# A decode block on one core: w_out's last rows cut into other lanes, x loaded row by row

## The chip, the core and the metric

The kernel runs on one core of a Trainium2 chip. The metric is the device time in microseconds. Before the change its median over three runs is 662.07 us (661.95 to 662.16).

## The reference

A decode step for four sequences (B = 4, one new token each, D = 640). The normalised x feeds two branches whose results are added to x: attention over a cache of 4,096 positions with 32 heads of 128, and a gated MLP with F = 1728, Fh = 864.

```python
def _A_ref(x, k_cache, v_cache, wq, wo):          # caches: (4, 32, 4096, 128) bf16
    q = (x @ wq).reshape(B, 1, 32, 128).transpose(0, 2, 1, 3)
    scores = jnp.einsum('bhqd,bhkd->bhqk', q, k) * Dh ** (-0.5)
    p = _softmax(scores, axis=-1)
    o = jnp.einsum('bhqk,bhkd->bhqd', p, v)
    return o.transpose(0, 2, 1, 3).reshape(B, 1, 4096) @ wo

def _B_ref(x, w_in, w_sp, b_sp, w_out):
    z = _gelu(jnp.einsum('bsd,df->bsf', x, w_in))
    z1, z2 = z[..., :Fh], _layernorm(z[..., Fh:], axis=-1)
    g = jnp.einsum('ts,bsf->btf', w_sp, z2) + b_sp[None, :, None]
    return jnp.einsum('bsf,fd->bsd', z1 * g, w_out)   # w_out: (864, 640)

xn = _layernorm(x, axis=-1)
return x + _A_ref(xn, k_cache, v_cache, wq, wo) + _B_ref(xn, w_in, w_sp, b_sp, w_out)
```

The two caches are 134 MB each; together with the weights 282 MB have to come in from HBM.

## The kernel before

**Units.** Attention is cut into NU = 16 units: a group of 8 heads of one sequence, 8 x 4096 rows of 128 as 128 partitions x 256 rows. A unit's k is 8.4 MB and its v as much. A unit's k is worked on in NK = 4 quarters of 64 rows per partition. The ring (`k_ring`) has 7 such places, `v_all` holds one unit's v.

**Steps.** For each quarter n: `product(n)` (L537) multiplies k by q on VectorE, `fold_half(n)` (L543) adds the halves, `sums(n)` (L555) lets TensorE add up the rest through the identity, `row_sums` (L569) finishes a score row. At the first quarter of the next unit come `head_max` (L578 to L588), `exps` (L596, ScalarE) and `by_head` (L607). `weighted` (L631) multiplies v by the probabilities. After every fourth unit `group_turn` and `group_proj` (L672 to L699) multiply by w_o into `out_ps`, where x and the MLP's result are summed as well.

**Loads.** All of them but x, w_sp and b_sp go out on SyncE's DMA queue, in the order of the list `loads` (L195). `pump()` issues the next one as soon as its places in ring or `v_all` are free by the program's order; the semaphores then hold it on the chip until the last reader is done. The list starts: wq (L118), k of unit 0 in quarters 0 and 1 (L164), `load_w` (w_in, L127, and w_out's parts with t = 1, L124), k of unit 0 in quarters 2 and 3, `load_w_few` (w_out's part with t > 1), k of unit 1. From there v and k alternate. Every DMA of the program, SyncE's and ScalarE's alike, takes one of eight semaphores in turn, so a DMA also waits until the one eight places earlier has landed.

**w_out.** `W_OUT` (L62) cuts its 864 rows into parts (partitions, rows per partition, transfers): 128 partitions of five rows (800 KB, in `v_all`), 128 of one row (160 KB) and 12 partitions, here called lanes, of eight rows (10,240 bytes each). The lanes go in four transfers of three lanes: `w[l:n:t]` with t = 4. `w_rows` lists the 14 row sets (NFC) with their first row, partitions and step.

**x.** One transfer of four rows on ScalarE's queue (L101), w_sp and b_sp after the first q (L735, L736).

**MLP.** `gmlp()` is a generator whose steps are called in the first two quarters: the products with w_in (L404), a copy of PSUM for each run of parts with the same number of partitions (`by_lanes`, L414), GELU, layer norm and gate (L418 to L500), and the products with w_out (L503), which read all parts. V of unit 0 (L175) is loaded into `v_all` after them.

**The end.** The last unit's v comes in two halves, the second cut into 32, 16, 8, 8 rows (`V_CUTS`), then w_o of the last group in six pieces (L228, L231); the last products (L809, L699), a copy on ScalarE (L823) and two transfers out (L824, L825) follow.

Of the kernel before, what the change touches and what calls it, by code (L numbers as in the profile page):

```python
# [10 lines left out]
BF16 = mybir.dt.bfloat16  # L11
# [6 lines left out]
def kernel(  # L18
# [14 lines left out]
    nc = tc.nc  # L33
    P = nc.NUM_PARTITIONS
    Bsz, Sq, D = A_x.shape
    _, H, S, Dh = A_k_cache.shape
    HD = A_wq.shape[1]
    F = B_w_in.shape[1]
    Fh = F // 2
# [19 lines left out]
    RW = 8  # L59
    QW = HC * Dh  # L60
    RING = 2 * NK - 1
    W_OUT = ((P, 5, 1), (P, 1, 1), (12, 8, 4))  # L62
    assert sum(n * r for n, r, _ in W_OUT) == Fh
    NFC = sum(r for _, r, _ in W_OUT)

    def up(n):
        return -(-n // 256) * 256

    PW = sum(up(r * D) for _, r, _ in W_OUT[1:])
    NOH = D // 2  # L70
    CB = 4
    NG = NR // CB
# [8 lines left out]
    const = ctx.enter_context(tc.tile_pool(name="const", bufs=1))  # L81
# [16 lines left out]

    ring = places.tile([P, RING, QW], BF16, name="k_ring")
    x_bf = ring[0:Bsz, 1, 0:D]  # L100
    nc.scalar.dma_start(out=x_bf, in_=A_x.flatten_outer_dims())  # L101
    v_all = places.tile([P, NK * QW], BF16, name="v_all")

    wq_sb = v_all[:, 0 : DC * HD].rearrange("p (c n) -> p c n", c=DC)
# [2 lines left out]

    at_v = up(DC * (HD + F))
    w_parts, f0, at_p = [], 0, 0
    for n, r, t in W_OUT:  # L110
        if f0 == 0:
            room = v_all[0:n, at_v : at_v + r * D]
        else:
            room = p_buf[0:n, at_p : at_p + r * D]
            at_p += up(r * D)
        w_parts.append((room.rearrange("p (k n) -> p k n", k=r), f0, n, r, t))
        f0 += n * r
    nc.sync.dma_start(out=wq_sb, in_=A_wq.rearrange("(p c) n -> p c n", c=DC))  # L118

    def load_part(part):  # L120
        w, f0, n, r, t = part
        rows = B_w_out[f0 : f0 + n * r].rearrange("(p k) n -> p k n", k=r)
        for l in range(t):
            nc.sync.dma_start(out=w[l:n:t], in_=rows[l:n:t])  # L124

    def load_w():
        nc.sync.dma_start(out=w_in_sb, in_=B_w_in.rearrange("(p c) n -> p c n", c=DC))  # L127
        for part in w_parts:
            if part[4] == 1:
                load_part(part)  # L130

    def load_w_few():
        for part in w_parts:
            if part[4] > 1:
                load_part(part)

    w_rows = [
        (w[:, i], f0 + i, n, r) for w, f0, n, r, _ in w_parts for i in range(r)
    ]

    def run_of(cache, u):
# [101 lines left out]
    for e in range(PAR):  # L243
        nc.gpsimd.tensor_copy(
            out=of_row[:, e, :, :, e, :],
            in_=ident[:].rearrange("p (k q) -> p q k", q=QD)[:, 0:Bsz, :, None].to_broadcast(
                [P, Bsz, NQ, LN]
            ),
# [15 lines left out]
    for i in range(NSTAT):  # L264
# [5 lines left out]
        out=rstd[:], in_=mv[:, 1:2], func=ACT.Sqrt, bias=eps_tile[:Bsz], scale=1.0  # L270
# [4 lines left out]
        out=xn_bf,  # L275
# [4 lines left out]
        op1=ALU.mult,  # L280
    )

    wsp_bf = const.tile([1, 1], BF16)
    bsp_bf = const.tile([1, 1], BF16)

    xn_v = xn_bf.rearrange("b (p c) -> b c p", c=DC)
    xnT_ps = ps_m.tile([P, DC, Bsz], BF16, tag="m")
    for c in range(DC):
        nc.tensor.transpose(
            out=xnT_ps[:, c, :], in_=xn_v[:, c, :], identity=ident[:Bsz, :Bsz]  # L290
# [8 lines left out]
    for e in range(PAR):  # L299
        q_ps = ps_pv.tile([P, HG, Dh], FP32, tag="pv", name="q_ps")  # L300
        for c in range(DC):
            for k in range(NQ):
                nc.tensor.matmul(  # L303
                    out=q_ps[k * QD : (k + 1) * QD],
# [5 lines left out]
        rows = const.tile([P, HG, Dh], BF16, name=f"q_rows{e}")  # L310
        nc.vector.tensor_scalar(  # L311
            out=rows[:], in0=q_ps[:], scalar1=scale_qk, scalar2=None, op0=ALU.mult
# [7 lines left out]
        out=hot[:].rearrange("p c h -> p (c h)"),  # L320
        in_=ident[:].rearrange("p (g m) -> p m g", m=QD),
# [6 lines left out]
        out=pick[:, :, Bsz - 1 :].rearrange("p c (k q) -> p c k q", q=QD)[  # L328
            :, :, :, 0 : PAR * Bsz : Bsz
        ],  # L330
        in_=hot[:].rearrange("p c (k e) -> p c k e", e=PAR),
# [4 lines left out]
        out=of_set[:],  # L336
        in_=hot[:].rearrange("p c h -> p (c h)")[:, 0 : PAR * Bsz].rearrange(
            "p (e b) -> p e b", b=Bsz
        ),
# [5 lines left out]
    with nc.allow_low_precision("0 and 1"):  # L345
        nc.vector.tensor_reduce(
            out=own[:],
            in_=ident[:].rearrange("p (h l) -> p h l", h=HT),
# [5 lines left out]
        out=par[:], in_=own[:].rearrange("p (k e) -> p e k", e=PAR), axis=AX.X, op=ALU.add  # L354
# [3 lines left out]
        out=far[:],  # L358
# [13 lines left out]
    for half in range(2):  # L372
        nc.tensor.matmul(
            out=out_ps[OG * half : OG * half + OG, :],
# [7 lines left out]
    for name in ("zz", "gw", "gt"):  # L382
        gm[name] = work.tile([P, 2, NFC, Bsz], FP32, name=name)
    gm["gz"] = work.tile([P, 3, NFC, Bsz], FP32, name="gz")
    nc.gpsimd.memset(gm["zz"][:], 0.0)
    gm["st"] = work.tile([1, 5 * Bsz], FP32, name="st")
    gm["ac"] = work.tile([1, 2 * Bsz], FP32, name="ac")
    gm["yT"] = work.tile([P, NFC, Bsz], BF16, name="yT")

    by_lanes = []  # L390
    for n, r, _ in W_OUT:
        if by_lanes and by_lanes[-1][0] == n:
            by_lanes[-1] = (n, by_lanes[-1][1] + r)
        else:
            by_lanes.append((n, r))

    def gmlp():
        zz, gw, gt, gz = (gm[n] for n in ("zz", "gw", "gt", "gz"))
        zT = ps_pv.tile([P, 2, NFC, Bsz], FP32, tag="pv", name="zT")
        for t in range(2):  # L400
# [331 lines left out]
    E = mybir.EngineType  # L732
    with tc.manual_schedule(engines={E.PE, E.DVE, E.Activation, E.SP}):
        stage_q(0)
        nc.scalar.dma_start(out=wsp_bf[:], in_=B_w_sp[0:1, 0:1])  # L735
        nc.scalar.dma_start(out=bsp_bf[:], in_=B_b_sp[0:1].rearrange("(a b) -> a b", a=1))  # L736
        waiting = None
        mlp = gmlp()
        for n in range(NK * NU):
            u, i = divmod(n, NK)  # L740
            product(n)
            if n and n % 2 == 0:
                row_sums(n - 1)
            if i == 0 and u:
                head_max(u - 1)
                if waiting in taken:
                    picked(waiting)
            fold_half(n)
            if n == 1:
                next(mlp)  # L750
                next(mlp)
            if i == 0 and u:
                exps(u - 1)
                if waiting in pvs:
                    take(waiting)
                by_head(u - 1)
            sums(n)
            if i == 0 and u + 1 < NU:
                stage_q(u + 1)
            if i == 0 and waiting is not None:  # L760
                if waiting in taken:
                    picked(waiting)
                if waiting % Bsz == Bsz - 1:
                    group_turn(waiting // Bsz)
                    group_proj(waiting // Bsz)
                waiting = None
            if n == 0:
                next(mlp)
            if n == 1:
                next(mlp)  # L770
                next(mlp)
                next(mlp)
                busy.remove(V)
            if n in turns:
                w = waiting = turns[n]
                if w % Bsz == Bsz - 1:
                    group_den(w // Bsz)
                if w == NU - 3:
                    weighted(w, v_runs[:, 0:NC], more=True)
                    weighted(w, v_runs[:, NC:NR], NG // 2)  # L780
                else:
                    weighted(w, v_runs)
                if i < NK - 1:
                    take(w)
                busy.remove(V)
            pump()
        weighted(NU - 2, v_runs)
        row_sums(NK * NU - 1)
        head_max(NU - 1)
        exps(NU - 1)  # L790
        take(NU - 2)
        by_head(NU - 1)
        den = ps_m.tile([P, NQ, PAR, Bsz], FP32, tag="m", name="den_all")
        nc.tensor.matmul(
            out=den[:],
            lhsT=ones_sq[:],
            rhs=acc[(HG - 1) % NACC][:, :, 0 : PAR * Bsz],
            start=True,
            stop=True,
        )  # L800
        rden = small.tile([P, NQ, PAR, Bsz], FP32, name="rden_all")
        nc.vector.reciprocal(out=rden[:], in_=den[:])
        picked(NU - 2)
        u, b = NU - 1, Bsz - 1
        weighted(u, v_ends[0])
        take(u)
        pick_last(u, more=True)
        for c in range(NC):
            nc.tensor.matmul(  # L809
                out=o_last[0][:, :, :, b],  # L810
                lhsT=v_ends[1][:, c, :],
                rhs=p_m[:, u % 2, NG // 2 + c // CB, c % CB, :].rearrange("p (k e) -> p k e", e=PAR),
                start=False,
                stop=(c == NC - 1),
            )
        o_n = small.tile([P, NQ, PAR, Bsz], BF16, name="o_n_last")
        nc.vector.tensor_tensor(out=o_n[:], in0=o_last[0][:], in1=rden[:], op=ALU.mult)  # L817
        gr[HG - 1] = [o_n[:, h // PAR, h % PAR, :] for h in range(HT)]
        group_proj(HG - 1)

        res = v_all[:, 0:NOH]
        out_v = out.flatten_outer_dims()
        nc.scalar.copy(out=res[0 : OG + Bsz], in_=out_ps[0 : OG + Bsz])  # L823
        nc.scalar.dma_start(out=out_v[:, 0:NOH], in_=res[0:Bsz])  # L824
        nc.sync.dma_start(out=out_v[:, NOH:D], in_=res[OG : OG + Bsz])  # L825
# [30 lines left out]
```

## Time and profile before

| what | us |
|---|---|
| median of three runs | 662.07 |
| the profiled execution's own time | 662.09 |
| its span, from first to last instruction | 660.2 |
| VectorE busy | 522.6 |
| TensorE busy (granted clock 0.692 over the span) | 317.0 |
| SyncE's queue, share of the 16 DMA engines | 99.1% |
| VectorE waiting for k before `product` | 87.9, in 13 waits, the longest 7.6 |
| issue of a whole unit's k to its landing, median | 27.2 |
| the same for v | 32.6 |

"Busy" is the time in which an engine worked on an instruction; issues of DMAs and semaphore work are not in it. The page also slices the span into 40 parts; the DMA's row, in tenths, is 9 in each but the last:

```profile
DMA  9999999999999999999999999999999999999997
GB/s 369 433 461 434 417 441 434 433 437 438 421 445 426 437 430 441 437 422 433 434 441 441 418 437 441 430 441 421 434 441 437 426 421 445 422 427 436 449 409 284
```

### The profile page before, as it was taken

What the parts mean: (1) busy time and instruction counts of PE and PEld (TensorE: products, weight loads), DVE (VectorE), ACT (ScalarE), POOL (GpSimd) and SP (SyncE); (2) the same over time, 40 slices, a digit from 0 to 9 for tenths busy, and PEclk for the clock granted to TensorE, in tenths of its full rate; (3) what the DMA queues carried; (4) which work ended last, traced back from release to release, by engine and by line L of the source; (5) the groups of instructions that cost most, each with busy time, mean ns of one, the idle gap of its engine ahead of it and who ended that gap; (6) DMA issues with size and microseconds to landing.
All of it is one profiled execution on the core that took longest, in us unless ns stands there. A gap on an engine that the chain in (4) does not pass through costs nothing.

```text
span 660.2 us, 4777 instructions
## 1 busy us (share of the span) xinstructions
PE 317.0 (48%) x2083; PEld 136.3 (21%) x2083; DVE 522.6 (79%) x276; ACT 29.9 (5%) x73; POOL 10.1 (2%) x20
## 2 busy tenths in 40 slices
PE   0574372526427363452636336263452534737367
PEld 0231121212213121120212112121120211212124
DVE  1767978959597795969959598695969969999950
ACT  0020000000000000000000000000000000000000
POOL 2300000000000000000000000000000000000000
PEclk9757676766767676585767768676685867676785
DMA  9999999999999999999999999999999999999997
GB/s 369 433 461 434 417 441 434 433 437 438 421 445 426 437 430 441 437 422 433 434 441 441 418 437 441 430 441 421 434 441 437 426 421 445 422 427 436 449 409 284
DMA packets 8232, 282.55 MB, mean 428 GB/s; under 512 B 892, under 2 KB 2184, under 8 KB 2568
## 3 DMA queue, kind: packets, MB, share of 16 engines
q1 hardware_dynamic: 8192, 282.25, 99.1%
q8 instruction: 16, 0.26, 0.1%
q10 hardware_dynamic: 20, 0.01, 0.0%
q14 instruction: 4, 0.03, 0.0%
HBM read 282.24 MB, written 0.01 MB: 428 GB/s over the span
## 4 chain that ended last, share of the span: by engine, by line
DMA 62%; DVE 28%; PE 8%; issue 1%; ACT 0%; DVEq 0%
DMA k_ring<-in_A_k_cache_dram 53%; DVE k_ring L537 14%; DVE k_ring L543 7%; PE s_ps L555 6%; DMA v_all<-in_A_v_cache_dram 4%; DMA k_ring<-in_A_wo_dram 3%; DVE s_sb L569 3%; DMA v_all<-in_A_wq_dram 2%; DVE p_m L607 1%; DVE m L578 1%; PE q_ps L303 1%; PE pv L631 1%; PE out_ps L699 1%; DVE p_m L678 1%; DVE mf L580 1%
## 5 line engine op out<-in xcount | busy, mean ns | idle before, releaser
L537 DVE TENSOR_TENSOR k_ring<-k_ring,qbc 128x8192 bf16<-128x8192 bf16 x64 | 282.9, 4420 | 88.5 <-DMA k_ring<-in_A_k_cache_dram 87.9
L555 PE MATMUL s_ps<-k_ring,ident 128*128 128x512 bf16 x512 | 202.2, 566 | 313.8 <-DVE k_ring L543 313.7
L555 PEld LDWEIGHTS <-ident 128*128 128x128 bf16 x512 | 64.0, 130 | 430.0 <-issue 245.4
L543 DVE TENSOR_TENSOR k_ring<-k_ring 128x4096 bf16<-128x4096 bf16 x64 | 145.9, 2280 | 1.1
L631 PE MATMUL pv<-v_all,p_m 128*32 128x512 bf16 x960 | 62.5, 419 | 0.0
L569 DVE TENSOR_REDUCE s_sb<-s_ps 128x128 f32<-128x1024 f32 x32 | 39.0, 1218 | 3.7 <-PE s_ps L555 3.7
L607 DVE TENSOR_TENSOR p_m<-p_c,own 128x2048 bf16<-128x2048 bf16 x16 | 36.6, 2285 | 0.7 <-ACT p_c L596 0.7
L631 PEld LDWEIGHTS <-p_m 128*32 128x32 bf16 x992 | 26.6, 106 | 42.5 <-issue 23.3
L596 ACT ACTIVATE p_c<-s_sb,nm 128x256 bf16<-128x256 f32 x16 | 8.1, 508 | 342.9 <-DVE nm L588 342.9
L662 PEld LDWEIGHTS o_ps<-o_rows,pick 128*128 128x128 f32 x96 | 20.4, 294 | 4.3 <-issue 3.3
L662 PE MATMUL o_ps<-o_rows,pick 128*128 128x128 f32 x96 | 19.1, 367 | 0.0
L643 ACT COPY o_rows<-pv 128x512 f32<-128x512 f32 x16 | 9.4, 586 | 165.7 <-PE pv L631 165.7
L311 DVE TENSOR_SCALAR q_rows<-q_ps 128x512 bf16<-128x512 f32 x2 | 1.4, 692 | 12.8 <-PE q_ps L303 12.8
L817 DVE TENSOR_TENSOR o_n_last<-o_last,rden_all 128x32 bf16<-128x32 f32 x1 | 0.2, 192 | 12.2 <-PE o_last L809 12.2
L303 PE MATMUL q_ps<-v_all,xnT 128*32 128x512 bf16 x40 | 4.5, 630 | 9.3 <-DMA v_all<-in_A_wq_dram 9.3
L527 ACT CAST qbc<-qbc_ps 128x128 bf16<-128x128 f32 x16 | 4.3, 266 | 97.6 <-PE qbc_ps L519 97.6
L578 DVE TENSOR_REDUCE m<-s_sb 128x1 f32<-128x256 f32 x16 | 6.7, 420 | 0.5
L519 PE MATMUL qbc_ps<-q_rows,of_row 128*128 128x128 bf16 x32 | 6.0, 276 | 0.6 <-DVE q_rows L311 0.6
L519 PEld LDWEIGHTS <-of_row 128*128 128x128 bf16 x32 | 4.1, 132 | 8.1 <-issue 7.4
L716 PE MATMUL o_last<-hot,o_rows 128*128 128x8 f32 x32 | 4.9, 279 | 0.7 <-ACT o_rows L643 0.7
L716 PEld LDWEIGHTS o_last<-hot,o_rows 128*128 128x128 f32 x32 | 4.8, 226 | 1.8 <-ACT o_rows L643 1.6
L699 PE MATMUL out_ps<-k_ring,p_m 128*4 128x320 bf16 x48 | 4.0, 309 | 2.1 <-DVE p_m L691 2.1
(87 smaller groups left out, 81.4 us busy)
## 6 DMA issues: line engine op xcount, KB each, us to landing
k_ring<-in_A_k_cache_dram SPq DMA_DIRECT2D x5, 4096.0 KB, 27.2
v_all<-in_A_v_cache_dram SPq DMA_DIRECT2D x2, 4096.0 KB, 28.2
v_all<-in_A_wq_dram SPq DMA_DIRECT2D x1, 5120.0 KB, 15.4
k_ring<-in_A_k_cache_dram SPq DMA_DIRECT2D x2, 2048.0 KB
k_ring<-in_A_v_cache_dram SPq DMA_DIRECT2D x1, 4096.0 KB
k_ring<-in_A_wo_dram SPq DMA_DIRECT2D x3, 1280.0 KB, 20.6
v_all<-in_B_w_in_dram SPq DMA_DIRECT2D x1, 2160.0 KB
k_ring<-in_A_v_cache_dram SPq DMA_DIRECT2D x1, 2048.0 KB
```

The lines of the kernel that those rows point to most:

```text
L303: nc.tensor.matmul(out=q_ps[k * QD : (k + 1) * QD], lhsT=xnT[:, c, :], rhs=wq_v[:, c, k, e], start=(c == 0), stop=(c == DC - 1),)
L519: nc.tensor.matmul(out=qb_ps[:], lhsT=of_row[:, e, b].rearrange("p k f l -> p (k f l)"), rhs=q_rows[e][:, hg, :], start=(e == 0), stop=(e ...
L537: nc.vector.tensor_tensor(out=t, in0=t, in1=qbcs[u][:, None, :].to_broadcast([P, HC, Dh]), op=ALU.mult)
L543: nc.vector.tensor_tensor(out=t[:, :, 0:HD2], in0=t[:, :, 0:HD2], in1=t[:, :, HD2:Dh], op=ALU.add)
L555: nc.tensor.matmul(out=s, lhsT=ident[:], rhs=t[:, :, g * RW : (g + 1) * RW], start=(g == 0), stop=(g == m - 1),)
L569: nc.vector.tensor_reduce(out=scores[u][:].rearrange("p (r c) -> p r c", r=NK)[:, lo : hi + 1 : hi - lo], in_=sums_ps.pop(n // 2)[:], axis ...
L578: nc.vector.tensor_reduce(out=m1[:], in_=scores[u][:], axis=AX.X, op=ALU.max)
L607: nc.vector.tensor_tensor(out=p_m[:, u % 2], in0=p_c.pop(u)[:].rearrange("p (g c) -> p g c", c=CB)[:, :, :, None].to_broadcast([P, NG, CB, HT]
L631: nc.tensor.matmul(out=pvs[u][cg * QD : (cg + 1) * QD, :], lhsT=p_m[:, u % 2, g0 + n].rearrange("p c h -> p (c h)"), rhs=v_at[:, n * CB : ...
L662: nc.tensor.matmul(out=gr[hg][:], lhsT=pick[:, c, Bsz - 1 - b : P + Bsz - 1 - b], rhs=o[:, c, :], start=(b == 0 and c == 0), stop=(b == Bs ...
L699: nc.tensor.matmul(out=out_sum(half), lhsT=o, rhs=wo_sb[:, n, half * NOH : (half + 1) * NOH], start=False, stop=(hg == HG - 1 and n == HT ...
L716: nc.tensor.matmul(out=o_last[0][:, :, :, u % Bsz], lhsT=o[:, c, :], rhs=hot[:, c, :].rearrange("p (k e) -> p k e", e=PAR), start=(c == 0) ...
```

## The change

`W_OUT` gets three other parts: 128 partitions of five rows as before, 24 partitions of one row, and 25 lanes of eight rows. A part now lists its transfers as (when, first lane, number of lanes, step): "wide" ones go out with `load_w`, "few" ones with `load_w_few`, and lane 22 goes in two halves of four rows, one with each. So 128 rows in one transfer and 96 rows in four become 24 rows in three transfers (12, 8 and 4 lanes) and 200 rows in eight: with `load_w` one of five lanes and half a lane, with `load_w_few` two of five, three of three and the other half lane. NFC stays 14. The flag `near` is true in every part, so each partition's rows stay neighbours in HBM.

x is loaded in four transfers of one row. The loads of w_sp and b_sp move from after the first q to right behind x on ScalarE's queue. `by_lanes` now has three runs of parts, so the copy at L414 is made three times. The steps of the MLP stand as they were, and so does everything behind it.

On SyncE's queue six transfers come in, four ahead of k's quarters 2 and 3 and two ahead of unit 1's k. With three more on ScalarE's, the turn of the eight semaphores moves, so the early loads wait for others than before: k's quarter 1 for x's first row, w_in for wq, the first half lane for k's quarter 0, k's quarters 2 and 3 for quarter 1, the six small transfers after it for w_in, w_out's five rows, and the 12-, 8-, 4- and 5-lane transfers, k of unit 1 for the first half lane.

```diff
-    W_OUT = ((P, 5, 1), (P, 1, 1), (12, 8, 4))
-    assert sum(n * r for n, r, _ in W_OUT) == Fh
-    NFC = sum(r for _, r, _ in W_OUT)
+    W_OUT = (
+        (P, 5, True, (("wide", 0, 128, 1),)),
+        (24, 1, True, (("wide", 0, 12, 1), ("wide", 12, 8, 1), ("wide", 20, 4, 1))),
+        (25, 8, True, (("wide", 1, 5, 4), ("few", 2, 5, 4), ("few", 7, 5, 4), ("few", 0, 3, 4), ("few", 3, 3, 9), ("few", 16, 3, 4), ("half", 22, 1, 1))),
+    )
+    assert sum(n * r for n, r, _, _ in W_OUT) == Fh
+    NFC = sum(r for _, r, _, _ in W_OUT)
...
-    nc.scalar.dma_start(out=x_bf, in_=A_x.flatten_outer_dims())
+    x_rows = A_x.flatten_outer_dims()
+    for b0, b1 in ((0, 1), (1, 2), (2, 3), (3, 4)):
+        nc.scalar.dma_start(out=x_bf[b0:b1], in_=x_rows[b0:b1])
+    wsp_bf = const.tile([1, 1], BF16)
+    bsp_bf = const.tile([1, 1], BF16)
+    nc.scalar.dma_start(out=wsp_bf[:], in_=B_w_sp[0:1, 0:1])
+    nc.scalar.dma_start(out=bsp_bf[:], in_=B_b_sp[0:1].rearrange("(a b) -> a b", a=1))
...
-    def load_part(part):
-        w, f0, n, r, t = part
-        rows = B_w_out[f0 : f0 + n * r].rearrange("(p k) n -> p k n", k=r)
-        for l in range(t):
-            nc.sync.dma_start(out=w[l:n:t], in_=rows[l:n:t])
+    def load_part(part, on):
+        w, f0, n, r, near, cuts = part
+        rows = B_w_out[f0 : f0 + n * r].rearrange(
+            "(p k) n -> p k n" if near else "(k p) n -> p k n", k=r
+        )
+        for kind, l, m, step in cuts:
+            if kind == on:
+                end = l + (m - 1) * step + 1
+                nc.sync.dma_start(out=w[l:end:step], in_=rows[l:end:step])
+            if kind == "half":
+                part_r = slice(0, r // 2) if on == "wide" else slice(r // 2, r)
+                nc.sync.dma_start(out=w[l : l + m, part_r], in_=rows[l : l + m, part_r])
 
     def load_w():
         nc.sync.dma_start(out=w_in_sb, in_=B_w_in.rearrange("(p c) n -> p c n", c=DC))
         for part in w_parts:
-            if part[4] == 1:
-                load_part(part)
+            load_part(part, "wide")
 
     def load_w_few():
         for part in w_parts:
-            if part[4] > 1:
-                load_part(part)
+            load_part(part, "few")
...
     w_rows = [
-        (w[:, i], f0 + i, n, r) for w, f0, n, r, _ in w_parts for i in range(r)
+        (w[:, i], f0 + i * (1 if near else n), n, r if near else 1)
+        for w, f0, n, r, near, _ in w_parts
+        for i in range(r)
     ]
...
         stage_q(0)
-        nc.scalar.dma_start(out=wsp_bf[:], in_=B_w_sp[0:1, 0:1])
-        nc.scalar.dma_start(out=bsp_bf[:], in_=B_b_sp[0:1].rearrange("(a b) -> a b", a=1))
```

More of the change, by code (lines that the diff above doesn't have):

```diff
@@ L61 @@
     RING = 2 * NK - 1
-    W_OUT = ((P, 5, 1), (P, 1, 1), (12, 8, 4))
-    assert sum(n * r for n, r, _ in W_OUT) == Fh
-    NFC = sum(r for _, r, _ in W_OUT)
+    W_OUT = (
[5 more added lines that the diff above has]
+    NFC = sum(r for _, r, _, _ in W_OUT)
     def up(n):
         return -(-n // 256) * 256
-    PW = sum(up(r * D) for _, r, _ in W_OUT[1:])
+    PW = sum(up(r * D) for _, r, _, _ in W_OUT[1:])
     NOH = D // 2
@@ L109 @@
     w_parts, f0, at_p = [], 0, 0
-    for n, r, t in W_OUT:
+    for n, r, near, cuts in W_OUT:
         if f0 == 0:
@@ L115 @@
             at_p += up(r * D)
-        w_parts.append((room.rearrange("p (k n) -> p k n", k=r), f0, n, r, t))
+        w_parts.append((room.rearrange("p (k n) -> p k n", k=r), f0, n, r, near, cuts))
         f0 += n * r
     nc.sync.dma_start(out=wq_sb, in_=A_wq.rearrange("(p c) n -> p c n", c=DC))
-    def load_part(part):
-        w, f0, n, r, t = part
-        rows = B_w_out[f0 : f0 + n * r].rearrange("(p k) n -> p k n", k=r)
-        for l in range(t):
-            nc.sync.dma_start(out=w[l:n:t], in_=rows[l:n:t])
+    def load_part(part, on):
[10 more added lines that the diff above has]
+                nc.sync.dma_start(out=w[l : l + m, part_r], in_=rows[l : l + m, part_r])
     def load_w():
@@ L281 @@
     )
-    wsp_bf = const.tile([1, 1], BF16)
-    bsp_bf = const.tile([1, 1], BF16)
     xn_v = xn_bf.rearrange("b (p c) -> b c p", c=DC)
@@ L390 @@
     by_lanes = []
-    for n, r, _ in W_OUT:
+    for n, r, _, _ in W_OUT:
         if by_lanes and by_lanes[-1][0] == n:
```

## The prediction

> **What bounds the kernel now.** I read the page's totals, then the chain that ended last, then SyncE's issues, then stretches of the span.
>
> ```profile
> span 660.2 us, 4777 instructions
> PE 317.0 (48%) x2083; PEld 136.3 (21%) x2083; DVE 522.6 (79%) x276; ACT 29.9 (5%) x73; POOL 10.1 (2%) x20
> DMA packets 8232, 282.55 MB, mean 428 GB/s; under 512 B 892, under 2 KB 2184, under 8 KB 2568
> q1 hardware_dynamic: 8192, 282.25, 99.1%
> q8 instruction: 16, 0.26, 0.1%
> ```
>
> VectorE is busy for 79%, but the one queue that SyncE feeds keeps the 16 DMA engines at work for 99.1%. The second kind to note is q8: sixteen instruction fetches that share the same engines.
>
> ```profile
> 604.05 4.08 PE pv L631 x61
> 608.15 25.93 DMA v_all<-in_A_v_cache_dram
> 634.09 21.98 DMA k_ring<-in_A_wo_dram
> 656.07 0.04 issue
> 656.11 1.29 PE out_ps L699 x8
> 657.43 0.42 ACT v_all L823
> ```
>
> The chain's end (start, length): two DMAs back to back, then eight matmuls and the copy out. Nothing that computes stands between 608 and 656 us; the last landing sets the end.
>
> ```profile
> 42.00:632.00 590.00, 280.46 (x1611) 115.89 (x1610) 496.89 (x236) 22.41 (x60) 0.00 (x0) 0.68 1.00 433
> 650.00:654.00 4.00, 3.38 (x127) 3.29 (x125) 0.00 (x0) 0.00 (x0) 0.00 (x0) 0.50 1.02 396
> 654.00:657.00 3.00, 2.48 (x24) 1.03 (x20) 0.19 (x1) 0.00 (x0) 0.00 (x0) 0.50 0.51 173
> ```
>
> Stretches of the span; the last two columns are the DMA's busy share and GB/s. The share is 1.00 for 590 us and halves only in the last three: some engines have finished, others have not.
>
> The trace also keeps each packet's start, length and size. A packet starts 4 ns before the end of its predecessor on the same engine (less for packets under 4 KB), so the packets can be strung into 16 chains. From 2.5 to 646 us no chain rests, the fetches apart. The kernel is therefore 16 queues that never rest, and it ends when the fullest is empty. I compare them where each finishes the last v unit's first half: from 640.23 to 643.43 us. Three groups explain the spread. Three chains carry four 10,240-byte packets each near 42 us (the four 3-lane transfers of w_out, one lane per engine, always the same three: call them the first three engines); they stand near 641.8, 641.9 and 642.3. Eight chains are hit by q8 fetches, in a fixed rotation and twice each. The packet after a fetch starts 0.86 us late and takes 2.97 instead of 2.42 us, so a fetch costs its engine 1.41 us. These eight stand at 642.8 to 643.4 (the one whose second fetch is at 654.56 counted with it; where two chains run in step, which of them a fetch hit is read from the rotation). The other five stand at 640.2 to 641.8. The latest, 643.43, is a fetch engine; its last packet ends at 656.62.
>
> **The change, part by part.** The bytes stay the same; what changes is who carries them. Prices from the packet records: a 10,240-byte packet 0.385 us, with its semaphore packet 0.39; a 1,280-byte packet every 0.052, alone with its semaphore 0.06; the old 128-row transfer 8 x 0.052 + 0.01 = 0.43 us on every engine. The trace shows n lanes on n engines only for three lanes; I carry it on to 12, 8, 5 and 4, counted from the same end.
>
> - Removed: 0.43 us on every engine; four lanes, 4 x 0.39 = 1.56, on the first three.
> - Added: three single rows on the first four engines (0.18), two on the next four (0.12), one on the next four (0.06), none on the last four. Lanes of eight: transfers of 5, 5, 5, 3, 3, 3 give six lanes (2.34) to the first three engines and three (1.17) to the fourth and fifth. The lane cut in halves: two 5,120-byte pieces, all on the first engine (0.39) or spread over all (0.02); I take the first, by the nearest row (one descriptor, one packet).
> - Net: engines 2 and 3 gain 2.34 + 0.18 - 1.56 - 0.43 = +0.53; engine 1 the same plus 0.39 and three more rows of x, 0.16, so +1.08; engines 4 and 5 +0.92 and +0.86; 6 to 8 -0.31; 9 to 12 -0.37; 13 to 16 -0.43.
>
> The eight fetch engines are none of the first three. Eight in a fixed rotation look like one half of the sixteen, hence the upper half, 9 to 16, and the five others would be 4 to 8. So the latest falls by 0.37 or 0.43; on 6 to 8 it would be 0.31. I take 0.37. Engine 1 rises from at most 641.94 to 643.02, just below 643.43 - 0.37 = 643.06. Engines 4 and 5 rise to at most 641.77 + 0.92 = 642.69.
>
> **What must stay covered.** Eight semaphores go round over all DMAs, so each waits for the one eight places earlier. Today:
>
> ```profile
> 0.73 0.39 SPq L118 DMA_DIRECT2D v_all<-in_A_wq_dram  x1
> 2.83 0.53 SPq L127 DMA_DIRECT2D v_all<-in_B_w_in_dram  x1
> 16.12 0.33 SPq L164 DMA_DIRECT2D k_ring<-in_A_k_cache_dram  x1
> 20.95 7.95 SPq L124 DMA_DIRECT2D p_m<-in_B_w_out_dram  x4
> 32.04 0.34 SPq L164 DMA_DIRECT2D k_ring<-in_A_k_cache_dram  x1
> ```
>
> Changed, in SyncE's order: k's second quarter waits for x's first row (3 us), w_in for wq (16.1), the first half lane for k's first quarter (20.9), k's second half for the second quarter (25.8, where a 3-lane transfer waits for it now, instead of 16.1). Behind it queue five lane transfers, the other half lane and k of unit 1. The engines then still hold w_in, 8 packets of 0.64 us, and w_out's five rows, 8 of 0.24: work until about 32.3. A first packet comes 1.0 us after issue (wq: 0.73 to 1.74), so 5.5 us are to spare. The next six issues wait for w_in (about 31) and w_out (about 32.9), then take 0.65 to 0.8 us each as in the x4 row: k of unit 1 is issued near 36.5, instead of 32.0. K's second half lasts until 41.3 or later, so 3.8 us are to spare: cost nothing. Uncovered, each microsecond without work would reach the end whole, since no chain rests later.
>
> The lanes land on the first engines near 44.3 us. VectorE's yT ends at 44.7, and the matmuls that read these rows follow the first ten, at 46.0; cover 1.7 us. Behind them waits v of unit 0 (46.29), and k of unit 1 keeps the engines busy until 61. x's last row lands near 5 instead of 3.0 us; x_n is needed when wq lands, at 16.1, and was ready at 7.2: 7 us of cover for a shift of 2. The third zz copy (0.16 us) and the moved w_sp and b_sp issues lie before 63 us, where VectorE waits for k: nothing.
>
> The tail follows the DMA: the 8 last matmuls start when w_o's fifth and sixth head land on the latest engine, and PE idles 0.6 us before the last v rows, so 0.37 us comes through whole. Sum: 662.09 (660.2 span, 1.9 around it) - 0.37 = 661.72. The profiled run is 0.02 above the median, so 661.7.
>
> One cost no row bounds from the code alone: the order of the first packets. The 16 first packets of wq take 1.5 to 2.8 us and leave lags of 14.5 to 15.8 at wq's end; the latest chain brings 15.17, about 0.5 behind the usual 14.7. Four issues for x may redraw this: between -0.5 and +0.6 (15.76 for 15.17); I take 0.
>
> [...]
>
> **Rivals.**
> 1. Slower: a fetch engine is the fourth or fifth. The latest could then rise by 0.92: 663.0. For it: packet records name no engine. Against: the rotation of eight, and five chains without fetch are left for places 4 to 8. It decides once such an engine stands above 642.5. Chance 0.10.
> 2. Slower by more: the queue runs dry before k of unit 1. It decides once that issue comes after 40.3. If each of the six waits for its forerunner's landing, as x took it (issue 0.73, VectorE starts 3.01: 2.28 us), it is at 32.9 + 13.7 = 46.6, first packet 47.6 against 41.3: +6.3, 668.0 with the gain. For it: one strictly ordered issuer with six waits. Against: the transfers they wait for were issued 15 us earlier, and the rows give 0.65 to 0.8 an issue. [...] Chance 0.04.
> 3. No gain: the first engine, fuller by 1.08, takes the latest's place (0.04 us below it in my sum), or the start lags do: 661.9 to 662.3. Chance 0.22.
> 4. More: the latest loses its start lag too: down to the next fetch engines, 643.12 - 0.37 = 642.75, or the first engine at 643.02; at most 0.87 gained, 661.2. Chance 0.12.
> 5. The change doesn't do what it says: single lanes spread over all engines. Then the first engine has 0.35 less; the end is as forecast.
>
> **How the numbers follow.** Forecast (661.5 to 661.9, rival 5 in it) 0.50; the cases above hold 0.48, and 0.02 stays for a gain I have not seen. The range for 8 in 10 takes rivals 3 and 4: 661.2 to 662.4. About 0.2%, 1.3 us, is what a measurement of this kernel can tell from no change: faster than 660.75 has 0.02, slower than 663.4 has 0.04, between them 0.94.
>
> **What would show it.** Right: no gap in the DMA share up to 640 us; k's second half issued near 25.8, k of unit 1 near 36.5; the last wait for w_o ending some 0.4 us earlier. Wrong: an issue of k of unit 1 after 40, a DMA share under 0.97 in 20 to 45 us, or a later landing of w_o without any gap (rivals 1 and 3).

## The result, and the profile after

The changed kernel took 663.24 us (median; 663.06 to 663.44), the kernel before, run beside it, 661.99 (661.74 to 662.19): a ratio of 1.0019, interval 1.0012 to 1.0025. The forecast was 661.7 with a range of 661.2 to 662.4, and the measured time lies above it: the change costs 1.25 us instead of gaining 0.37. That is small, 0.19%, but the interval leaves out 1, so it is a slowdown and not noise. The profiled execution took 663.44 us, with a span of 661.3 (before: 662.09 and 660.2).

The page's totals of the changed kernel, then the end of its chain of waits (start, length):

```profile
span 661.3 us, 4796 instructions
PE 314.6 (48%) x2083; PEld 136.7 (21%) x2083; DVE 522.6 (79%) x277; ACT 29.8 (5%) x73; POOL 4.2 (1%) x20
q1 hardware_dynamic: 8124, 282.25, 99.1%
```

```profile
608.27 26.90 DMA v_all<-in_A_v_cache_dram
635.19 21.97 DMA k_ring<-in_A_wo_dram
657.16 0.04 issue
657.20 1.32 PE out_ps L714 x8
658.54 0.42 ACT v_all L836
```

The share of SyncE's queue is the same 99.1%, the same bytes move, and VectorE is busy for the same 522.6 us. The chain has the same form too: w_o's last wait takes 21.97 us (21.98 before), but it begins at 635.19 instead of 634.09, and w_o lands at 657.16 instead of 656.07. The whole 1.1 us is there before the tail begins. So the DMA engines, which the share calls equally busy, have become later without resting.

The stretches of the span show where. Columns as before; the last is GB/s. This view counts a packet where it starts, which is why a share can pass 1. First the changed kernel, then the kernel before:

```profile
41.00:48.00 7.00, 4.58 (x12) 1.65 (x12) 3.09 (x16) 1.96 (x4) 0.00 (x0) 0.52 1.11 426
48.00:60.00 12.00, 5.60 (x36) 2.22 (x37) 11.81 (x7) 1.37 (x2) 0.00 (x0) 0.63 1.00 433
```

```profile
41.00:48.00 7.00, 5.99 (x32) 2.33 (x32) 4.62 (x8) 1.45 (x2) 0.00 (x0) 0.50 1.06 458
48.00:60.00 12.00, 5.04 (x17) 1.67 (x14) 11.00 (x5) 0.00 (x0) 0.00 (x0) 0.64 1.00 433
```

From 48 us on both move 433 GB/s. From 41 to 48 the changed kernel moves 426 where the kernel before moved 458, at a share that is no lower (1.11 against 1.06). Engines that are busy and move less have slower packets. The packet records say which: the kernel before writes all twelve lanes of w_out in packets of 385 ns and all the 65,536-byte packets of unit 1's k beside them in 2,418 ns. In the changed kernel the lanes that start up to 42.4 us take 385 ns, and the nine that start from 42.6 to 44.2 take 441 to 691; the k packets that start from 41 to 48 us take up to 3,468. Taking each packet's length over the median of its size as lost, 14.66 us are lost over all engines between 40 and 45 us (0 before), about 0.9 us on each of the 16; it is not only the engines that carry lanes.

### The profile page after: what moved, and what is told of

Same layout as the page of the kernel before. It is cut to its first block, busy times and chain, and to the rows that moved or that the text cites. A ratio compares the mean times of both kernels' runs of the same rounds, so it can differ in the third digit from the quotient of the medians.

```text
span 661.3 us, 4796 instructions
## 1 busy us (share of the span) xinstructions
PE 314.6 (48%) x2083; PEld 136.7 (21%) x2083; DVE 522.6 (79%) x277; ACT 29.8 (5%) x73; POOL 4.2 (1%) x20
## 3 DMA queue, kind: packets, MB, share of 16 engines
q1 hardware_dynamic: 8124, 282.25, 99.1%
## 4 chain that ended last, share of the span: by engine, by line
DMA 64%; DVE 27%; PE 7%; issue 1%; SPq 1%; ACT 0%; DVEq 0%
DMA k_ring<-in_A_k_cache_dram 52%; DVE k_ring L552 13%; DVE k_ring L558 6%; PE s_ps L570 6%; DMA v_all<-in_A_v_cache_dram 4%; DMA k_ring<-in_A_wo_dram 3%; DVE s_sb L584 3%; DMA v_all<-in_B_w_out_dram 2%; DMA v_all<-in_A_wq_dram 2%; DVE p_m L622 1%; DVE m L593 1%; PE out_ps L714 1%; DVE p_m L693 1%; PE pv L646 1%; DVE mf L595 1%
## 5 line engine op out<-in xcount | busy, mean ns | idle before, releaser
L646 PE MATMUL pv<-v_all,p_m 128*32 128x512 bf16 x960 | 59.6, 405 | 0.0
L622 DVE TENSOR_TENSOR p_m<-p_c,own 128x2048 bf16<-128x2048 bf16 x16 | 36.5, 2284 | 0.7 <-ACT p_c L611 0.7
L419 PE MATMUL zT<-xnT,v_all 128*25 128x4 bf16 (+2 forms) x140 | 6.4, 183 | 0.0
L419 PEld LDWEIGHTS <-v_all 128*25 128x25 bf16 (+2 forms) x140 | 6.3, 134 | 0.0
```

The source lines that it names most:

```text
L419: nc.tensor.matmul(out=zT[0:n, t, k, :], lhsT=w_t[:, c, f : f + (n - 1) * r + 1 : r], rhs=xnT[:, c, 0:Bsz], start=(c == 0), stop=(c == DC ...
L622: nc.vector.tensor_tensor(out=p_m[:, u % 2], in0=p_c.pop(u)[:].rearrange("p (g c) -> p g c", c=CB)[:, :, :, None].to_broadcast([P, NG, CB, HT]
L646: nc.tensor.matmul(out=pvs[u][cg * QD : (cg + 1) * QD, :], lhsT=p_m[:, u % 2, g0 + n].rearrange("p c h -> p (c h)"), rhs=v_at[:, n * CB : ...
```

## The experiments

Each kernel was timed over five rounds against the kernel before on the same chip.

**Which half of the change: x_alone and w_alone.** The first is the kernel before with x in four rows and the early loads of w_sp and b_sp; the second is the changed kernel without these, so only w_out's parts differ from before.

```diff
 x_alone, against the kernel before
-    nc.scalar.dma_start(out=x_bf, in_=A_x.flatten_outer_dims())
...
+    for b0, b1 in ((0, 1), (1, 2), (2, 3), (3, 4)):
+        nc.scalar.dma_start(out=x_bf[b0:b1], in_=x_rows[b0:b1])
...
+    nc.scalar.dma_start(out=wsp_bf[:], in_=B_w_sp[0:1, 0:1])
...
 w_alone, against the changed kernel
...
-    for b0, b1 in ((0, 1), (1, 2), (2, 3), (3, 4)):
-        nc.scalar.dma_start(out=x_bf[b0:b1], in_=x_rows[b0:b1])
...
+    nc.scalar.dma_start(out=x_bf, in_=A_x.flatten_outer_dims())
...
```

> The kernel before with only x in four rows and w_sp, b_sp moved up. In the changed kernel's packet records every engine loses some 0.8 us between 42.4 and 45 us, where nothing was lost before. Theory P (place): that stretch is there because lanes of w_out are written to partitions which in 128-partition transfers other engines write; x has no part in it. Then here: x lands near 14 us, no slow stretch, 662.0 +- 0.3. Rival Q (lateness): late x shifts the MLP by 4 us into the stretch where lanes and unit 1's k land, and that slows the engines. Then here: the slow stretch, 662.8 or more.

> The changed kernel with x in one transfer of four rows and w_sp, b_sp where they were. Theory P: the slow stretch stays, 0.6 to 1.4 us lost on each engine, 662.9 to 663.3. Rival Q: no slow stretch, and the gain that the sum forecast, 661.6.

w_alone took 663.23 us (663.08 to 663.35; ratio 1.0019, interval 1.0010 to 1.0028): the whole slowdown, with 13.4 us lost over all engines (engine-us) between 40 and 45 us. x_alone took 662.34 (662.15 to 662.52; 1.0006, interval 0.9997 to 1.0014), with no lengthened packet in that stretch and w_o landing at 656.00 as before. Whether x's rows cost the 0.38 us that its median shows is not settled; put on top of w_alone they add nothing (663.24 against 663.23), and on top of lanes28, below, 0.07.

**What makes the packets slow: own and cross.** Both have x as before and the same parts: five rows on 128 partitions, 64 single rows in one transfer, 20 lanes of eight in four transfers of five lanes. They differ only in which five lanes go together: every fourth one (step 4) or five neighbours (step 1).

```diff
 own, against the changed kernel
-        (24, 1, True, (("wide", 0, 12, 1), ("wide", 12, 8, 1), ("wide", 20, 4, 1))),
-        (25, 8, True, (("wide", 1, 5, 4), ("few", 2, 5, 4), ("few", 7, 5, 4), ("few", 0, 3, 4), ("few", 3, 3, 9), ("few", 16, 3, 4), ("half", 22, 1, 1))),
+        (64, 1, True, (("wide", 0, 64, 1),)),
+        (20, 8, True, (("few", 0, 5, 4), ("few", 1, 5, 4), ("few", 2, 5, 4), ("few", 3, 5, 4))),
...
 cross, against own
-        (20, 8, True, (("few", 0, 5, 4), ("few", 1, 5, 4), ("few", 2, 5, 4), ("few", 3, 5, 4))),
+        (20, 8, True, (("few", 0, 5, 1), ("few", 5, 5, 1), ("few", 10, 5, 1), ("few", 15, 5, 1))),
```

With a step of 4 the five lanes of each transfer, one per engine, go to partitions l, l+4, l+8, l+12, l+16: the first engine always writes partitions 0 to 3, the second 4 to 7, and so on. With a step of 1 each transfer goes to five neighbouring partitions, so up to four engines write into one group of four. That the trace's first engine carries the first lane of a transfer, and so on, is taken from the order: packet records name neither engine nor partition. The four partitions that step 4 gives an engine in this order are called its own below. Theory P holds that a transfer over 128 partitions gives it the same four; that was the author's assumption, no record shows it.

> [...] Theory P: no slow stretch; the fetch engines carry 0.21 us less (four single rows for eight), the fourth and fifth engine 1.35 more and stay below them: 661.8. Rival N (number): five engines with lanes beside unit 1's k slow everything, wherever the lanes go: slow stretch, 662.5 or more. Rival Q: 661.8.

> As the run before in every size and order, but each transfer of five takes five neighbouring lanes (step 1), so that up to four engines write to one group of four partitions. Theory P: lane packets take several times 0.385 us, and the other engines lose time too: 663 or more. Rivals N and Q: the same time as with step 4 within 0.2 us.

own took 662.09 us (661.89 to 662.22; 1.0002, interval 0.9994 to 1.0011), cross 664.10 (663.90 to 664.26; 1.0032, interval 1.0019 to 1.0045). Their stretches, own first:

```profile
41.00:48.00 7.00, 5.99 (x24) 2.10 (x22) 3.80 (x12) 1.87 (x4) 0.00 (x0) 0.50 1.09 469
48.00:60.00 12.00, 5.84 (x26) 2.03 (x25) 11.97 (x5) 0.00 (x0) 0.00 (x0) 0.62 0.99 427
```

```profile
41.00:48.00 7.00, 5.90 (x22) 2.14 (x22) 3.49 (x12) 2.18 (x4) 0.00 (x0) 0.50 1.11 385
48.00:60.00 12.00, 6.35 (x28) 2.11 (x27) 11.97 (x5) 0.00 (x0) 0.00 (x0) 0.50 1.00 433
```

385 GB/s against 469, with TensorE's and VectorE's columns alike. In own all 20 lanes take 385 ns and every k packet 2,418. In cross 18 of 20 lanes are stretched, the longest to 1,242 ns, and the first k packets of nine engines, all without a lane, take 3,805 to 3,893 ns, about 62% of the speed. 24.6 engine-us are lost, 1.5 per engine, and w_o lands 1.9 us later, as the chains of the two say (own first):

```profile
634.03 21.96 DMA k_ring<-in_A_wo_dram
```

```profile
635.88 21.97 DMA k_ring<-in_A_wo_dram
```

**Source or destination: own_near and cross_far.** The step changes two things, the rows in HBM and the partitions. These two kernels part them: own's partitions filled from five neighbouring lanes' rows in HBM, and cross's partitions filled from every fourth. They leave out the right order of w_out's last 160 rows, so the MLP's part of the sum is another; number, sizes and order of the transfers are the same.

```diff
 own_near, against own
-                nc.sync.dma_start(out=w[l:end:step], in_=rows[l:end:step])
+                src = slice(l, end, step) if on == "wide" else slice(l * 5, l * 5 + 5)
+                nc.sync.dma_start(out=w[l:end:step], in_=rows[src])
 cross_far, against cross
-                nc.sync.dma_start(out=w[l:end:step], in_=rows[l:end:step])
+                src = slice(l, end, step) if on == "wide" else slice(l // 5, 20, 4)
+                nc.sync.dma_start(out=w[l:end:step], in_=rows[src])
```

> The run with four transfers of five lanes at step 4, whose lanes go to the same partitions, but each transfer takes five neighbouring lanes of HBM (so w_out's last 160 rows stand in the wrong lanes and the MLP's part of the sum is another). Theory P (place in SBUF): no slow stretch, lane packets 0.385 us, within 0.2 us of 662.09. Rival H (HBM): neighbouring rows read by five engines at once are what slowed the run with step 1: near 664.

> The run with step 1, whose lanes go to five neighbouring partitions, but each transfer takes every fourth lane of HBM (again w_out's last 160 rows in the wrong lanes). Theory P: the slow stretch stays, lane packets of 0.5 to 1.2 us, 664.1 +- 0.3. Rival H: 662.1.

own_near took 662.13 us (1.0003, interval 0.9994 to 1.0012), with all lanes at 385 ns and no loss from 41 to 45 us; cross_far 663.87 (1.0030, interval 1.0019 to 1.0041), with lanes up to 1,320 ns and k packets near 4,060. The time goes with the partitions that are written, not with the rows that are read.

**No wide transfer of single rows: lanes28 and lanes28_x.** If only the place counts, 28 lanes on partitions 0 to 27, one group of four per engine on seven engines, collide with nothing and take the old 128-row transfer (0.43 us) off the other nine. lanes28_x adds x's four rows.

```diff
 lanes28, against the kernel before
-    W_OUT = ((P, 5, 1), (P, 1, 1), (12, 8, 4))
+    W_OUT = ((P, 5, 1), (28, 8, 4))
```

> The kernel before with all 224 last rows in 28 lanes of eight, four transfers of seven lanes with step 4 (so each engine writes its own four partitions), no 128-row transfer. Theory P: no slow stretch anywhere; nine engines, the eight fetch engines among them, carry 0.43 us less; the fourth to seventh engine carry 1.13 more and stay under the latest: 661.96 - 0.4 = 661.55. Rival N (number of engines with lanes): seven of them slow everything: above 662.5.

> The same with x in four rows and w_sp, b_sp moved up. If the four rows of x cost what the run with them alone measured (+0.38, its interval just touching none): 0.3 to 0.5 above the same kernel with x in one transfer. If that was the start order of the first packets alone: between -0.2 and +0.5, without a rule.

662.87 us (662.72 to 663.06; 1.0015, interval 1.0006 to 1.0023) and 662.94 (1.0015, interval 1.0006 to 1.0024). No lane and no k packet is lengthened, and yet it is slower. The chains show another cause: in lanes28 two of the seven lane engines are also among the eight that are hit by two q8 fetches each. They carry four lanes (1.56 us) without the 0.43 and pay the fetches too, so they stand at 643.98 and 644.17 us at the end of the last v unit's first half, where the latest engine of the kernel before stands at 643.43. The lanes of own reach only five engines, none of which has a q8 fetch. So the sixth and seventh engines are fetch engines, or at least two of the engines that a seven-lane transfer reaches and a five-lane one does not.

**Lanes on the first five engines alone, in their own places: far5.** To load only engines without fetches, the 224 rows become 32 lanes of seven rows, 20 on partitions 0 to 19 in transfers of five, 12 on partitions 32 to 43 in transfers of three. The MLP then reads 12 row sets instead of 14.

```diff
 far5, against the kernel before
-    W_OUT = ((P, 5, 1), (P, 1, 1), (12, 8, 4))
+    LANES = ((0, 20, 5), (32, 12, 3))
+    LR = 7
...
+            for l in range(4):
+                if ((p0, l) in ((0, 0), (0, 1))) == (which == "wide"):
+                    nc.sync.dma_start(
+                        out=w_lanes[p0 + l : p0 + n : 4], in_=rows[l:n:4]
+                    )
...
```

> Edit: x, w_sp and b_sp as before; no 128-row transfer and no single rows. The 224 rows behind the five of each partition become 32 lanes of seven rows: 20 on partitions 0 to 19 in four transfers of five (step 4), 12 on partitions 32 to 43 in four transfers of three (step 4); the first two five-lane transfers go with w_in, the other six before unit 1's k. So the first three engines carry eight lanes each, the fourth and fifth four, all others none. Place theory (a lane slows everybody when its partition is served by another engine in wide transfers; partitions 0 to 19 and 32 to 43 are those of the same first engines; the first five engines have no instruction fetch): no packet is lengthened, each fetch engine carries 0.43 us less than before (8 x 0.052 + 0.01), the first engines 8 x 0.34 - 1.56 - 0.43 = +0.7 more and the fourth and fifth at most +0.9, all still below the fetch engines; w_o lands near 655.6 instead of 656.0 to 656.1, time 661.4 to 661.8, faster than before and after. Rival one (partitions 32 to 43 are other engines' places): the twelve lanes there collide as in the kernel with neighbouring lanes, 10 KB lanes stretched and every engine some 0.5 to 1.5 us late: 662.3 to 663.5. Rival two (number of lanes or of transfers counts, not their place): eight lanes on an engine are more than the six of after, so no less than after's 663.2.

All 32 lanes take 338 ns and all k packets beside them 2,418; w_o lands at 655.63, 0.44 us before the kernel before's 656.07, and neither rival's loss appears:

```profile
633.65 21.98 DMA k_ring<-in_A_wo_dram
655.63 0.04 issue
```

That fits partitions 32 to 43 belonging to the first three engines, as the place theory assumed, and eight lanes on each of them harm no other. It doesn't prove it: if lanes disturbed only each other, two engines writing lanes into one group at a time, far5 would come out the same, since no two of its engines do so. What the runs show is that lanes dealt with step 4 over partitions 0 to 19 and 32 to 43 lengthen nothing (338 ns here, 385 in own), and neighbouring lanes do (up to 1,242 ns in cross).

The time is 661.71 us (661.45 to 662.72) against 661.84 (661.70 to 662.39) of the kernel before in the same session, a ratio of 0.9998 with an interval of 0.9989 to 1.0007. The median span of the 11 runs is 659.8 us, of the 15 runs before 660.0. The landing moved as the sum has it, but what is left of it at the end is not to be told from nothing in the time: 0.44 us is a fifteenth of a per cent. It is the lowest median here, about 1.4 us below the changed kernel when each is taken against the kernel before of its session (1.25 + 0.13), but no shown gain on the kernel before.

## Why the prediction was wrong

**The step that failed: the price of a lane.** The sum gives a lane one price, 0.385 us (0.39 with its semaphore packet), paid by the engine that carries it and by no other, wherever the lane goes, and lists what each of 16 independent queues gains and loses. The row behind this price was the four 3-lane transfers, and all four of them put engine i's lane on engine i's own partitions (step 4). The changed kernel has five transfers of which that is not true: lanes 7, 11, 15, 19, 23 (one group of four too high for each engine), 3, 12, 21, then 16, 20, 24, and the two halves of lane 22 on the first engine. The slow stretch falls among these, but does not begin with the first of them: of lanes 7, 11, 15, 19 and 23 four still take 385 ns (in w_alone all five), and inside the stretch lanes in their own places (0 and 3) are lengthened too. So the cost is not one that a misplaced lane pays by itself. Whether a lane disturbs k's stream into the same group, or only another lane that is written there at the same time, as 7 and 4 are here, no run separates. Another 0.8 engine-us go near 32 us, where the single rows land, but only 0.06 in w_alone with the same rows. What the sum lacked is this one term: +0.83 us on nearly every engine that carries no lane (unit 1's k takes 20.15 instead of 19.31 us there).

**The latest engine.** The forecast had it fall by 0.37. Much of what was forecast did come, and is seen before the stretch: the semaphore packets that close k's second half on the first nine lane-free engines come at 41.1 to 41.7 us instead of 41.4 to 41.9, 0.2 to 0.4 earlier. Then the engine that was hit by a fetch at 39.15 us, in front of the stretch, loses 1.41 us in it (a 32,768-byte packet takes 1,620 instead of 1,213 ns and the next, of 65,536, 3,421 instead of 2,418). It is the latest from there to the end: its last packet ends at 657.69 instead of 656.62, -0.4 + 1.41 gives +1.0 of the +1.07 measured. Why this engine loses more than the other lane-free ones no run shows. No rival held this mechanism. The text did name its sign, "a later landing of w_o without any gap", but put it down to a fuller engine (rivals 1 and 3).

**The order of the issues** was right. SyncE's issues in the changed kernel (start, length):

```profile
16.02 0.33 SPq L144 DMA_DIRECT2D v_all<-in_B_w_in_dram  x1
...
20.84 0.24 SPq L141 DMA_DIRECT2D p_m<-in_B_w_out_dram  x1
25.71 0.35 SPq L181 DMA_DIRECT2D k_ring<-in_A_k_cache_dram  x1
30.88 4.82 SPq L138 DMA_DIRECT2D p_m<-in_B_w_out_dram  x5
35.74 0.41 SPq L141 DMA_DIRECT2D p_m<-in_B_w_out_dram  x1
36.29 0.36 SPq L181 DMA_DIRECT2D k_ring<-in_A_k_cache_dram  x1
```

K's second half went out at 25.71 us (forecast 25.8), the six small transfers from 30.88 on, about 0.9 us each, k of unit 1 at 36.29 (forecast 36.5), and no engine rested before it landed. Rival 2, the dry queue, fell with that: the nine more transfers left no engine idle. The half lane went whole to the first engine, as taken (one 5,120-byte packet each, 196 and 244 ns).

**x** was mis-sized, without effect. Forecast to land near 5 us, it was there only for the first statistics:

```profile
13.88 0.87 DVE L282 BATCH_NORM_STATS2 stats<-k_ring 4x6 f32<-4x320 bf16 x2 [13.88 <-DMA k_ring<-in_A_x_dram]
```

All four rows went to one engine, at 1.67, 5.69, 8.77 and 11.85 us, the last three each behind two packets of wq. The first `product` came at 23.90 instead of 21.95 us and yT at 48.6 instead of 44.5; all that lay under DMAs that never rested, and w_alone, without it, is no faster.

**Fetch engines.** That they were the upper half of the sixteen was a guess from their number, and lanes28 speaks against it. The first engine's rise (rival 3) and a fourth or fifth engine with fetches (rival 1) were not what decided: far5 puts more lanes on these engines (eight of 338 ns for six of 385, four for three) and is no slower.

**What stays open.** The runs show that the partitions decide (own_near 662.13 us, cross_far 663.87); why they do, none shows. Why crossed lanes slow all 16 engines (about 0.9 us each in the changed kernel), and not only those that meet, is as open; in cross, engines without any lane went down to 62% of their speed, 3,805 to 3,893 ns for a packet of 2,418.

## What to carry to other kernels

Where the DMA engines bound a kernel, as here at 99.1%, it is worth trying which partitions a transfer over few of them gives to each engine: here a step of 4 from partition 0 took 662.09 us, and a step of 1 664.10, 2 us more; no other step was compared by itself. A price read from one row holds only for what that row had in common with the new case: here the four old transfers put every lane on its engine's own partitions (385 ns each), and five of the new ones did not (lanes in and beside these took up to 691). And a busy share of 1 or more does not say that the engines move what they can: from 41 to 48 us it was 1.11 at 426 GB/s in the changed kernel and 1.06 at 458 before. Compare GB/s, or the length of packets of one size, before and after.

## What was not expected of the hardware

- A few crossed packets of 10,240 bytes slow engines that carry none of them: in cross the first 65,536-byte packets of nine engines go from 2,418 to some 3,885 ns.
- Packets are also lengthened beside the single rows: beside own's transfer of 64 rows, four per engine on neighbouring partitions, they gain 2.7 engine-us from 31.5 to 33.2 us, 0.17 us on each engine. That may be what uses up the 0.21 us that half the old 128 rows had cost, and w_o landed at 655.99 against 656.07 before. The size is not firm: beside the same transfer own_near lost 5.0 in that stretch, and w_o landed at 656.28. Dealt out in order, the 64 rows never put two engines into one group of four, so the account of the lanes does not explain it, and no run shows what does.
- The four transfers of one row of x, from one queue, did not spread: all went to one engine, at 1.67, 5.69, 8.77 and 11.85 us.
